# Top-k attention into an exact-GELU MLP: v's loads divided over the DMA queue, and three products of the last rows moved inside their slots

## The chip, the cores and the metric

The kernel runs on one core of a Trainium2 chip. The metric is the device time of one execution in microseconds (us). Five engines work side by side, each on its own list of instructions in order: TensorE (PE in the profile, with weight loads as PEld), VectorE (DVE), ScalarE (ACT), GpSimd (POOL) and SyncE (SP), which in this kernel issues nearly all DMAs. Waits between engines are semaphores. The time before is the median of three runs, 1484.7 us (1484.23 to 1486.39).

## The reference

```python
# q, k, v: (8, 8, 576, 64) float32;  w_in: (512, 2048);  w_out: (2048, 512)
scores = (q @ k.transpose(0, 1, 3, 2)) / np.sqrt(64)
kth = np.partition(scores, -32, axis=-1)[..., -32:-31]
scores = np.where(scores >= kth, scores, -1e9)
attn = np.exp(scores - scores.max(-1, keepdims=True))
attn = attn / (attn.sum(-1, keepdims=True) + 1e-9)
x = (attn @ v).transpose(0, 2, 1, 3).reshape(4608, 512)
h = x @ w_in
out = (0.5 * h * (1.0 + erf(h / np.sqrt(2.0)))) @ w_out
```

Each row of 576 scores keeps its 32 largest, the softmax runs over these, the result is multiplied with v, and the 4608 rows of all heads go through an MLP with exact GELU. All of it is float32.

## The kernel before

**Items and slots.** The heads of a batch are taken in four pairs. The 576 query rows of a pair are cut into four blocks of 128 rows (t = 0 to 3, "main") and 64 rows left over. The left-over rows of two pairs make one item together (t = 4, "last rows"). So a batch has 16 main items and 2 items of last rows, and the kernel has 144 items. In an even batch the last rows stand at the end, in an odd batch at the beginning, so four items of last rows follow one another: 16, 17, 18, 19, then 52 to 55, 88 to 91 and 124 to 127. The list `starts` holds the first item of each batch (54, 90 and 126 among them).

The main loop is software-pipelined over slots n = 0, 1, 2, ... . Slot n computes the scores of item n + 2 or n + 3 (`scores`, TensorE, copied out by ScalarE), finds the 32nd largest of item n (`top_k`, VectorE: MAX8 and MATCH_REPLACE8), masks and exponentiates item n - 1 (`softmax`, ScalarE, with its select at line 532 and its exponential at line 544), normalises item n - 1 (`normalise`, GpSimd, line 567), turns P of item n - 2 so that keys stand on partitions, multiplies P with v for an item some slots back (`attend`), and runs pieces of the MLP (`mlp`) in between.

**Two ways to turn P.** Most odd items are turned by TensorE (`transposes`, tiles tp and tp_t, copied to tile pt by ScalarE). From item 27 on, the last rows and most even items are `squared`: VectorE turns 32 x 32 squares in place (`square_p`, line 591), four DMAs write the item to a DRAM tile turned (`write_p`, line 601), and four DMAs read it back into pt (`read_p`, line 611). All of them are issued by SyncE in the order of the program. Tile pt has one buffer and holds two items side by side, the even one in the first half of its columns. A read for an even item therefore needs the products of the two items before it done. `delayed(i)` is true for squared last rows: items 52 to 55, 88 to 91 and 124 to 127.

**The products.** `attend(i)` multiplies pt with v. For main rows (line 727) one product covers two items, 256 columns. For last rows (line 738) it covers one item: two pairs of heads, 40 matmuls of 64 columns. The four products of a group of last rows are called first to fourth here (items 52, 53, 54, 55 in the first group). The result stands in a PSUM bank o and is copied to xT by ScalarE (lines 732 and 748). In this part of the kernel o, t_ps, tp_t and seven take turns in one single bank (tag "z"), so each waits until ScalarE has emptied the one before. Before the change the third and fourth product share one bank o and are copied to xT together.

Where the products stand before the change: the first at the beginning of slot 56 (n - 4 = 52), the second in slot 57 behind `softmax`, the third and fourth one after the other in slot 59, behind three pieces of the MLP. Slot 60 has the product of items 56 and 57.

**v.** Four buffers raw_v hold the v of four pairs; v0 to v3 stand for them here. The first product uses v0 and v1 for the last time in an even batch, the second v2 and v3; the third and fourth use what is loaded into these buffers for the next batch. One pair's `load("v", ...)` is four DMAs (lines 134 and 138). `issue` holds them back: in a slot with `held` set they go out at `flush()`, behind `write_p`.

**The MLP.** `l1_piece` (line 790) multiplies xT with w_in into h_ps; `gelus` applies GELU on ScalarE (line 806), with a table load because softmax's exponential needs another table; `sums` makes sums of GELU's output on GpSimd (lines 827 to 830). The second product of the MLP is done in seven products per pair of units: `seven_piece` (line 944, tile seven) and six in `trio_piece` (line 946, tiles y_ps). A "piece" is one entry of the list that `mlp` works through in order.

The slot's order around the change, shortened:

```python
mid = [i for i in (n - 5, n - 4) if delayed(i) and n % 2 and (i % 2 or i in starts)]
if not mid:
    read_p(n - 3)
...
if delayed(n - 4) and n % 2 == 0 and n - 4 not in starts:
    product = attend(n - 4)
...
if few[0]:
    softmax(n - 1, 0)
    if len(mid) == 1:
        mids()          # slot 57: second product, then read_p(54)
    if n % 2:
        mlp(ODD)        # ODD = 2 pieces
    if len(mid) == 2:
        mlp(1)
        mids()          # slot 59: third and fourth product, then read_p(56)
```

Of the kernel before, what the change touches and what calls it, by code (L numbers as in the profile page):

```python
# [14 lines left out]
def kernel(  # L15
# [19 lines left out]
    nc = tc.nc  # L35
# [5 lines left out]
    B, H, S, D = q.shape  # L41
# [4 lines left out]
    NP = H // 2  # L46
    NM = S // P
    SM = NM * P
    TL = S - SM
# [44 lines left out]
            return raws[n][pair % 2 if pair < SQUARES else 0]  # L94
        return raws[n][pair % len(raws[n])]

    held, late_issues = [False], []

    def issue(f):

        if held[0]:
            late_issues.append(f)
        else:
            f()
# [146 lines left out]
    items, starts = [], []  # L251
# [22 lines left out]
    def bank(name):  # L274

        tag = "z" if few[0] else ("z", "y0", "y1", "y2")[turn[0] % 4]
        turn[0] += 1
        return ps.tile([P, 512], f32, tag=tag, bufs=1, name=name)
# [298 lines left out]
    def delayed(i):  # L577

        return squared(i) and items[i][1] == NM
# [111 lines left out]
    def copy_x():  # L691
        while copies:
            copies.pop()()
# [2 lines left out]

    copies = []

    shared = []

    def column(tok):

        at = tok % RING
# [2 lines left out]
    def attend(i):  # L706

        if i < 0 or i >= N:
            return False
        pair, t = items[i]  # L710
        b, at = divmod(pair, NP)
        if t < NM and t % 2 == 0:
            return False
        pt = pt_now[0]
        both = delayed(i) and i - 1 in starts
        o = shared.pop() if both else bank("o")
        off = 2 * TL if both else 0
        n, row = (2 * P, (t - 1) * P) if t < NM else (TL, SM)
        tok = place_of(b, row)
        gap = RING if t == NM else COLS if tok % RING >= COLS else RING - COLS  # L720
        assert read[0] >= tok - gap + n
        c = slice(column(tok), column(tok) + n)
        if t < NM:
            vt = raw_of("v", pair)
            for j in range(NJ):
                for e in range(2):
                    nc.tensor.matmul(  # L727
                        o[e * D : (e + 1) * D, 0:n], lhsT=vt[:, j, e, :],
                        rhs=pt[:, e * NJ + j if j < NM else NM, :],
                        start=(j == 0), stop=(j == NJ - 1),  # L730
                    )
            copies.append(lambda: nc.scalar.copy(out=xT[:, at, c], in_=o[:, 0:n]))
        else:
            for r in range(2):
                vt = raw_of("v", pair + r)
                for j in range(NJ):
                    for e in range(2):
                        nc.tensor.matmul(
                            o[e * D : (e + 1) * D, off + r * TL : off + (r + 1) * TL],
                            lhsT=vt[:, j, e, :],  # L740
                            rhs=pt[:, e * NJ + j if j < NM else NM, i % 2 * P :][:, half(r, e)],
                            start=(j == 0), stop=(j == NJ - 1),
                        )
            if delayed(i) and i in starts:
                shared.append(o)
            else:
                first = 0 if both else at
                copies.append(lambda: nc.scalar.copy(
                    out=xT[:, first : at + 2, c],
                    in_=o[:, 0 : off + 2 * TL].rearrange("p (r n) -> p r n", n=TL),  # L750
                ))

        if t == (NM if b % 2 == 0 else NM - 1):
            for r in range(2 if t == NM else 1):
                issue(lambda r=r: load("v", pair + r + NP))
        if at == (NP - 1 if t < NM else NP - 2):
            assert n_tok[0] == tok
            n_tok[0] = tok + n
        return True
# [414 lines left out]
    for n in range(ahead):  # L1174

        held[0] = n < N and squared(n - 2)
        mid = [i for i in (n - 5, n - 4) if delayed(i) and n % 2 and (i % 2 or i in starts)]
        if not mid:
            read_p(n - 3)

        def mids():
            for i in mid:
                attend(i)
            copy_x()
            read_p(n - 3)
        left[0] = room_in(n)
        few[0] = n > START + 2
        eager[0] = n > N
        left[0] += closes(n - 3) - closes(n - 2)
        if not waits(unit_in(n)):  # L1190
            weights_add(unit_in(n))
        if n > 0:
            larger(n + 1)
        for piece in squares_in.pop(n, []):
            piece()
        if n == 1:

            for e in range(2):
                select(0, e)
            for e in range(2):  # L1200
                softmax(0, e)
        two = few[0] and n % 2 == 0 and n + 3 < N and items[n + 3][1] < NM
        scores(n + 2, two)
        if two:
            scores(n + 3)
        if delayed(n - 4) and n % 2 == 0 and n - 4 not in starts:
            product = attend(n - 4)
        else:
            product = not delayed(n - 3) and attend(n - 3)
        late = n > START  # L1210
        if n != 1 and n < START:

            for e in range(2):
                select(n - 1, e)
            softmax(n - 1, 0)
        copy_x()
        if n == START:

            for e in range(2):
                select(n - 1, e)  # L1220
            softmax(n - 1, 0)
        if waits(unit_in(n)):
            weights_size(unit_in(n))
            weights_add(unit_in(n))
        mlp(1)
        if closes(n - 3):
            ready[0] = n_tok[0]
        if few[0] and n % 2:
            run_gelus()
        tr = transposes(n - 2)  # L1230
        if product and n > START and done[0] < len(pieces) and pieces[done[0]][0] > ready[0]:

            for piece in tr[:1]:
                piece(n + 2 if few[0] else None)
            tr, ready[0] = tr[1:], n_tok[0]
        if not few[0] and n > START:
            softmax(n - 1, 0)
        mlp(1)
        if n != 1 and not late:
            softmax(n - 1, 1)  # L1240
        if few[0]:
            softmax(n - 1, 0)
            if len(mid) == 1:
                mids()
            if n % 2:
                mlp(ODD)
            if len(mid) == 2:
                mlp(1)
                mids()
        mlp(1)  # L1250
        prep = prep_in.pop(n, [])
        if n == 0:
            weights_size(unit_in(1))
            keep_busy(14, ident)
        if n == START + 1:

            for piece in prep:
                piece(None)
            prep = []
        if len(prep) > 1 and len(tr) == 3:  # L1260
            tr, prep = tr[:1] + prep[:1] + tr[1:], prep[1:]
        now = tr[:-1]
        if few[0]:
            now, tr, prep = tr + prep[:1], [], prep[1:]
        for x, piece in enumerate(now):
            piece(n + 2 if few[0] else None)
            ready[0] = n_tok[0]
            if few[0] and x == 2:
                break
            mlp(1)  # L1270
        ready[0] = n_tok[0]
        if late:
            softmax(n - 1, 1)
        if n > 0:
            smaller(n + 1)
        add_small(n - 1)
        for piece in tr[-1:] + prep:
            piece(None)
            mlp(1)
        if n < START:  # L1280

            keep_busy(4 if n == 0 else 8 if product else 14 if n < 5 else 18, ident)

        run_gelus()
        mlp(left[0])
        run_gelus()
        if n < N:
            top_k(n, lambda: inverse(n - 1), lambda: square_p(n - 2))
            write_p(n - 2)
            flush()  # L1290
            if n == 0:
                larger(1)
        else:
            inverse(n - 1)
        threshold(n)
        if n == 0:
            smaller(1)
        normalise(n - 1)
        sum_up(n + 2)
        if n in sums_in:  # L1300
            weight_sums(sums_in[n])
        run_small(6)

        if n > 0 and not waits(unit_in(n + 1)):
            weights_size(unit_in(n + 1))
        run_stores()
        if n == N:
            run_stores()
        for m in (n + 1, n + 2):

            if m > 2 and waits(unit_in(m)) == (m == n + 1):
                load_weights(m)
        if n < NP:
            load("v", n)
        if n == 5:
            nc.vector.memset(flat["k"][0][TL:, 0:TL], 0.0)
            load("q", SQUARES)
            load("k", SQUARES)
# [38 lines left out]
```

## Time and profile before

| | before |
|---|---|
| median of 3 runs | 1484.7 us (1484.23 to 1486.39) |
| the profiled execution: time, span | 1488.04 us, 1486.3 us |
| mean granted TensorE clock | 0.996 |
| busy share: PE, PEld, DVE, ACT, POOL | 98%, 77%, 88%, 73%, 77% |
| DMA writes of P (turned) / reads of P (pt), issues of 144 KB each | 240 / 240 |
| DMA loads of v, issues | 64 of 128 KB, 64 of 16 KB |

How to read the profile. A row of the timeline gives the start in us from the span's start, the length, the engine, the line of the kernel, the operation with its tiles (out<-in) and how many instructions are merged in it; brackets give the engine's idle time ahead of it and what ended that. SPq is SyncE's queue: its rows are the issues of DMAs, not the transfers. A row of the windows gives, for each stretch, its length, the busy time of each engine, the granted clock (1.00 is full speed) and the DMA engines' share. Buffer numbers are left out of tile names. A wait for several semaphores is put down to the one that came last.

### The profile page before, as it was taken

To read this page: it belongs to the slowest core of one execution; us is meant where nothing else is said; L and a number is where in the kernel's file an instruction comes from. 1 tells how busy PE (TensorE), PEld (TensorE's weight loads), DVE (VectorE), ACT (ScalarE), POOL (GpSimd) and SP (SyncE) were. 2 spreads that over 40 slices of the span, in tenths; PEclk is the share of its full clock that TensorE was granted. 3 is DMA by queue.
4 is the path that set the end of the run, shared out by engine and by line. 5 is a ranking of instruction groups with operands and counts; after the bars stand their busy time and mean duration, and the time that the engine had idled before them with its cause. 6 is when DMAs were issued, how large, how long until landed. Compare 5 with 4: busy or idle time off the path is not lost. (4 is left out here: it accounts for less than half of the span.)

```text
span 1486.3 us, 26513 instructions
## 1 busy us (share of the span) xinstructions
PE 1453.6 (98%) x8693; PEld 1137.4 (77%) x8693; DVE 1307.9 (88%) x3331; ACT 1081.5 (73%) x1899; POOL 1141.0 (77%) x1290
## 2 busy tenths in 40 slices
PE   8999999999999998999999999999999999899998
PEld 6776677887777776887777777787777777687787
DVE  7999899999999998899999999799999999898701
ACT  7999877877777775777777777677777777677620
POOL 6877567778888878777898978687788888877632
PEclk9999999999999999999999999999999999999999
DMA  7425210055434355245534337344443424623300
GB/s 195 144 86 131 76 47 1 23 100 100 88 82 86 62 108 128 59 95 112 104 79 85 72 67 155 67 94 96 97 101 74 88 63 93 130 60 73 66 15 15
DMA packets 544714, 127.05 MB, mean 85 GB/s; under 512 B 466464, under 2 KB 536128, under 8 KB 544576
## 3 DMA queue, kind: packets, MB, share of 16 engines
q1 hardware_dynamic: 543312, 124.93, 39.4%
q8 instruction: 69, 1.13, 0.3%
q14 instruction: 69, 0.57, 0.1%
q10 hardware_dynamic: 1200, 0.39, 0.1%
q0 software_dynamic: 64, 0.03, 0.0%
HBM read 80.47 MB, written 44.83 MB: 84 GB/s over the span
## 5 line engine op out<-in xcount | busy, mean ns | idle before, releaser
L790 PE MATMUL h_ps<-xT,w_in_sb 128*128 128x256 f32 (+1 forms) x2560 | 533.9, 361 | 0.0
L790 PEld LDWEIGHTS h_ps<-xT,w_in_sb 128*128 128x128 f32 x2560 | 438.5, 191 | 73.4 <-issue 25.5
L498 DVE MAX8 top<-lists 128x8 f32<-128x576 f32 (+1 forms) x792 | 475.8, 640 | 0.0
L501 DVE MATCH_REPLACE8 lists<-top,lists 128x288 f32<-128x288 f32 (+1 forms) x528 | 307.8, 589 | 0.0
L567 POOL TENSOR_TENSOR s<-s,stat 128x1152 f32<-128x1152 f32 x135 | 285.9, 2117 | 0.3 <-DVE stat L519 0.3
L532 ACT ACTIVATE s<-s,stat 128x576 f32<-128x576 f32 x288 | 224.9, 790 | 19.3 <-POOL stat L512 19.2
L544 ACT ACTIVATE s<-s,stat 128x576 f32<-128x576 f32 x288 | 225.0, 785 | 11.6 <-POOL lists L462 0.7
L525 POOL TENSOR_SCALAR stat<-stat 128x2 f32<-128x2 f32 x144 | 31.4, 218 | 218.7 <-ACT s L544 204.6
L470 POOL TENSOR_TENSOR lists<-lists 128x576 int32<-128x576 int32 x132 | 186.2, 1411 | 4.0
L462 POOL TENSOR_TENSOR lists<-s 128x576 int32<-128x576 int32 x133 | 187.6, 1411 | 0.0
L727 PE MATMUL o<-pt,raw_v 128*64 128x256 f32 x1280 | 154.0, 386 | 6.2 <-DMA pt<-turned 4.4
L727 PEld LDWEIGHTS o<-pt,raw_v 128*64 128x64 f32 x1280 | 87.6, 137 | 91.1 <-issue 44.1
L806 ACT ACTIVATE g<-h_ps 128x512 f32<-128x512 f32 x144 | 78.2, 595 | 108.7 <-PE h_ps L790 108.5
L946 PE MATMUL y_ps<-w_out_sb,sum 128*128 128x256 f32 x472 | 141.1, 381 | 0.0
L410 ACT ACTIVATE s<-s_ps 128x1024 f32<-128x1024 f32 x127 | 125.3, 1032 | 8.8 <-PE s_ps L402 8.2
L402 PE MATMUL s_ps<-kt,qm 64*128 64x512 f32 x512 | 129.4, 618 | 0.8 <-ACT s L408 0.8
L672 ACT COPY pt<-tp 128x1024 f32<-128x1024 f32 x73 | 74.3, 1018 | 57.5 <-PE tp L657 57.4
L501 DVE MATCH_REPLACE8 lists<-first,lists 128x288 f32<-128x288 f32 x264 | 114.3, 439 | 0.0
L946 PE MATMUL y_ps<-w_out_sb,g 128*128 128x256 f32 x480 | 113.7, 380 | 0.0
L519 DVE RECIPROCAL stat<-stat 128x2 f32<-128x2 f32 x144 | 22.9, 159 | 102.6 <-POOL stat L525 101.8
L498 DVE MAX8 first<-lists 128x8 f32<-128x288 f32 x268 | 106.6, 436 | 0.0
L437 DVE TENSOR_TENSOR lists<-s 128x576 f32<-128x576 f32 x133 | 101.0, 760 | 0.0
(162 smaller groups left out, 2489.0 us busy)
## 6 DMA issues: line engine op xcount, KB each, us to landing
turned<-s SPq DMA_DIRECT2D x240, 144.0 KB, 3.6
pt<-turned SPq DMA_DIRECT2D x240, 144.0 KB, 3.2
raw_v<-in_v_dram SPq DMA_DIRECT2D x64, 128.0 KB, 2.6
raw_q<-in_q_dram SPq DMA_DIRECT2D x112, 72.0 KB, 2.4
raw_k<-in_k_dram SPq DMA_DIRECT2D x112, 72.0 KB, 2.4
out_dram<-y SPq DMA_DIRECT2D x30, 256.0 KB, 2.1
w_out_sb<-in_moe_w_in_dram SPq DMA_DIRECT2D x14, 511.8 KB, 4.8
w_out_sb<-in_moe_w_out_dram SPq DMA_DIRECT2D x10, 511.8 KB, 4.1
```

Source lines behind the costliest of these rows:

```text
L402: nc.tensor.matmul(s_ps[:, e], lhsT=q_t[rows, :], rhs=kt[rows, main_keys(pair)], start=True, stop=True)
L410: nc.scalar.activation(spread(s, S + TL, SM), s_ps, func=AF.Copy, scale=scale)
L462: nc.gpsimd.tensor_tensor(t[:, :, 1].bitcast(i32), a.bitcast(i32), b.bitcast(i32), op=ALU.add)
L470: nc.gpsimd.tensor_tensor(into_of(i)[:, :, 1].bitcast(i32), both, top, op=ALU.subtract)
L498: nc.vector.max(x[:, e], src[:, e])
L501: nc.vector.match_replace(dst[:, e], x[:, e], src[:, e], LOWEST)
L532: nc.scalar.activation(s, s, func=AF.Prelu, bias=st["neg"][:, e : e + 1], scale=1.0, alpha=STEEP)
L544: nc.scalar.activation(s, s, func=AF.Exp, bias=st["bias"][:, e : e + 1], scale=1.0, accum_out=st["den"][:, e : e + 1],)
L567: nc.gpsimd.tensor_tensor(s, s, wide, op=ALU.mult)
L727: nc.tensor.matmul(o[e * D : (e + 1) * D, 0:n], lhsT=vt[:, j, e, :], rhs=pt[:, e * NJ + j if j < NM else NM, :], start=(j == 0), stop=(j = ...
L790: nc.tensor.matmul(h_tile(u)[:, i, :], lhsT=w_in_sb[:, ko, f * P : (f + 1) * P], rhs=xT[:, ko, c0 : c0 + n], start=(ko == 0), stop=(ko == ...
L946: nc.tensor.matmul(acc[names][:, k], lhsT=lhsT, rhs=rhs, start=(j == 0 and k == 0), stop=(j == FT // 2 - 1 and k == 1),)
```

## The change

In the slots of last rows (56, 57 and 59, and their like in the other two groups):

- v0's loads, and v2's, go out right behind the product that used the buffer last (`soon`, `issue_soon`), and not behind the write of P at the slot's end. v1's and v3's stay there. In slot 56 the read of P of item 53 now stands behind the first product and v0's loads; in slot 57 v2's loads stand behind the read of item 54.
- The second product (slot 57) stands behind two more pieces of the MLP (`mlp(ODD)`).
- The third product (slot 59) stands at the slot's beginning, in front of the last four h matmuls of its unit and of seven. The fourth stands behind two pieces, where three were.
- The third and fourth product no longer share a bank; each is copied to xT by itself.

On SyncE's queue the order per group was: write 53, read 53, write 54, v0, v1, read 54, write 55, v2, v3, stores, read 55, write 56, read 56. It is now: write 53, v0, read 53, write 54, v1, read 54, v2, write 55, v3, stores, read 55, write 56, read 56. TensorE runs the same matmuls; ScalarE has one copy more per group.

```diff
-    held, late_issues = [False], []
+    held, late_issues, soon = [False], [], []
+
+    def issue_soon():
+        while soon:
+            soon.pop()()
...
-        both = delayed(i) and i - 1 in starts
-        o = shared.pop() if both else bank("o")
-        off = 2 * TL if both else 0
+        o = bank("o")
...
-            if delayed(i) and i in starts:
-                shared.append(o)
-            else:
-                first = 0 if both else at
-                copies.append(lambda: nc.scalar.copy(
-                    out=xT[:, first : at + 2, c],
-                    in_=o[:, 0 : off + 2 * TL].rearrange("p (r n) -> p r n", n=TL),
-                ))
+            copies.append(lambda: nc.scalar.copy(
+                out=xT[:, at : at + 2, c],
+                in_=o[:, 0 : 2 * TL].rearrange("p (r n) -> p r n", n=TL),
+            ))
...
             for r in range(2 if t == NM else 1):
-                issue(lambda r=r: load("v", pair + r + NP))
+                f = lambda r=r: load("v", pair + r + NP)
+                if r == 0 and delayed(i):
+                    soon.append(f)
+                else:
+                    issue(f)
...
-        if not mid:
+        even_last = delayed(n - 4) and n % 2 == 0 and n - 4 not in starts
+        if not mid and not even_last:
             read_p(n - 3)
 
         def mids():
-            for i in mid:
-                attend(i)
-            copy_x()
-            read_p(n - 3)
+            attend(mid.pop(0))
+            if not mid:
+                copy_x()
+                read_p(n - 3)
+                issue_soon()
...
-        if delayed(n - 4) and n % 2 == 0 and n - 4 not in starts:
+        if even_last:
             product = attend(n - 4)
+            issue_soon()
+            read_p(n - 3)
         else:
             product = not delayed(n - 3) and attend(n - 3)
+        if len(mid) == 2:
+            mids()
...
             softmax(n - 1, 0)
-            if len(mid) == 1:
-                mids()
             if n % 2:
                 mlp(ODD)
-            if len(mid) == 2:
-                mlp(1)
-                mids()
+                if mid:
+                    mids()
```

More of the change, by code (lines that the diff above doesn't have):

```diff
@@ L697 @@
     copies = []
-    shared = []
     def column(tok):
@@ L738, in attend @@
                         nc.tensor.matmul(
-                            o[e * D : (e + 1) * D, off + r * TL : off + (r + 1) * TL],
+                            o[e * D : (e + 1) * D, r * TL : (r + 1) * TL],
                             lhsT=vt[:, j, e, :],
```

## The prediction

> **What bounds the kernel now.** I read the page's first part, then stages by windows, then TensorE's timeline where it waits.
>
> ```profile
> PE 1453.6 (98%) x8693; PEld 1137.4 (77%) x8693; DVE 1307.9 (88%) x3331; ACT 1081.5 (73%) x1899; POOL 1141.0 (77%) x1290
> ```
>
> ```profile
> 600.00:890.00 290.00, 289.56 (x1648) 226.89 (x1647) 272.32 (x702) 217.25 (x385) 237.47 (x266) 1.00 0.43 84
> 589.00:595.60 6.60, 6.60 (x33) 4.80 (x34) 6.60 (x15) 1.91 (x4) 6.52 (x8) 0.74 0.36 56
> 932.00:942.10 10.10, 10.09 (x71) 7.72 (x71) 2.83 (x7) 3.44 (x8) 0.71 (x1) 0.69 0.40 88
> 1291.00:1296.00 5.00, 5.00 (x33) 3.96 (x34) 5.00 (x14) 1.96 (x5) 4.92 (x5) 1.00 0.01 3
> ```
>
> Columns: stretch, its length, busy time of PE, PEld, DVE, ACT and POOL, granted clock, DMA. Between two groups of last rows TensorE is busy 289.56 of 290.00 us: what it gains inside a group isn't given back behind it. In two of the three groups the clock falls (0.74, 0.69). The change touches slots 56, 57 and 59 and their like (items 52 to 55, 88 to 91, 124 to 127). TensorE in the first group:
>
> ```profile
> 544.91 1.39 PE L738 MATMUL o<-pt,raw_v 128*64 128x64 f32 x40
> 555.06 1.39 PE L738 MATMUL o<-pt,raw_v 128*64 128x64 f32 x40 [0.58 <-ACT y L962]
> 559.30 0.49 PE L367 MATMUL t_ps<-kt,qm 128*128 128x128 f32 x2
> 565.42 6.21 PE L790 MATMUL h_ps<-xT,w_in_sb 128*128 128x256 f32 x28
> 572.63 1.13 PE L944 MATMUL seven<-w_sum,g 128*128 128x256 f32 x4 [1.00 <-POOL g L829]
> 573.60 1.89 PE L946 MATMUL y_ps<-w_out_sb,g 128*128 128x256 f32 x8
> 575.32 0.59 PE L946 MATMUL y_ps<-w_sum,sum 128*128 128x256 f32 x2
> 578.90 1.39 PE L738 MATMUL o<-pt,raw_v 128*64 128x64 f32 x40 [1.24 <-DMA pt<-turned]
> 580.22 0.70 PE L946 MATMUL y_ps<-w_sum,sum 128*128 128x256 f32 x2
> 581.18 0.38 PE L367 MATMUL tp_t<-kt,qm 128*128 128x128 f32 x2
> 588.95 3.47 PE L727 MATMUL o<-pt,raw_v 128*64 128x256 f32 x20 [2.75 <-DMA pt<-turned]
> ```
>
> 544.91, 555.06 and 578.90 are the first, second and fourth product; the third stands just before the fourth. 588.95 is the product of items 56 and 57, the first after the group. Four waits: 0.58, 1.00, 1.24, 2.75. The other groups:
>
> ```profile
> 923.98 1.13 PE L944 MATMUL seven<-w_sum,g 128*128 128x256 f32 x4 [0.99 <-POOL g L829]
> 932.01 2.40 PE L738 MATMUL o<-pt,raw_v 128*64 128x64 f32 x40 [2.99 <-DMA pt<-turned]
> 942.16 2.38 PE L727 MATMUL o<-pt,raw_v 128*64 128x256 f32 x20
> 1275.53 1.13 PE L944 MATMUL seven<-w_sum,g 128*128 128x256 f32 x4 [0.99 <-POOL g L829]
> 1282.09 1.39 PE L738 MATMUL o<-pt,raw_v 128*64 128x64 f32 x40 [1.51 <-DMA pt<-turned]
> 1290.99 2.38 PE L727 MATMUL o<-pt,raw_v 128*64 128x256 f32 x20 [1.61 <-DMA pt<-turned]
> ```
>
> The waits for P sum to 1.24 + 2.75 + 2.99 + 1.51 + 1.61 = 10.10 us. Who makes P late is in the DMA queue's own timeline, first group:
>
> ```profile
> 541.61 3.70 SPq L601 DMA_DIRECT2D turned<-s  x4
> 547.94 2.54 SPq L611 DMA_DIRECT2D pt<-turned  x4
> 550.71 3.54 SPq L601 DMA_DIRECT2D turned<-s  x4
> 554.36 0.78 SPq L134 DMA_DIRECT2D raw_v<-in_v_dram  x1
> 560.55 2.78 SPq L611 DMA_DIRECT2D pt<-turned  x4
> 563.43 3.37 SPq L601 DMA_DIRECT2D turned<-s  x4
> 566.85 0.95 SPq L134 DMA_DIRECT2D raw_v<-in_v_dram  x1
> 572.50 1.00 SPq L861 DMA_DIRECT2D out_dram<-y  x2
> 573.56 2.59 SPq L611 DMA_DIRECT2D pt<-turned  x4
> 576.26 3.42 SPq L601 DMA_DIRECT2D turned<-s  x4
> 583.78 2.54 SPq L611 DMA_DIRECT2D pt<-turned  x4
> ```
>
> These are write 53, read 53, write 54, eight loads of v (v0, v1), read 54, write 55, eight loads (v2, v3), stores, read 55, write 56, read 56. From 550.71 to 576.26 the queue issues without a break, so issuing, not moving, makes read 55 late; eight loads cost 560.55 - 554.36 = 6.19 or 572.50 - 566.85 = 5.65, four about 2.9. Before read 53 it stands free from 545.31 to 547.94: read 53 waits for write 53 to land.
>
> **The change part by part.** In the changed program the order per group is: write 53, four loads (v0), read 53, write 54, four (v1), read 54, four (v2), write 55, four (v3), stores, read 55, write 56, read 56. As many issues as before; 24 of them, four loads in each of six places, stand earlier.
>
> *v0's loads* wait on the queue for the first half of the first product (544.91 + 0.66 = 545.6); read 53 and write 54 stand behind them. They fill 545.7 to about 548.6, mostly the free stretch, so read 53 starts 0.7 us later; write 54, which needs VectorE's square only, moves from 550.71 to about 551.4. v1's follow to 557.9. Read 54 needs write 54 landed (read 53 followed its write by 547.94 - 541.61 = 6.33: 557.7) and the second product done, since P's buffer is single (below: 557.5): it starts near 557.9, not 560.55. v2's loads come at 560.7, write 55 stays at about 563.6, v3's run from 567.0 to 569.8, and after 1.06 for the stores read 55 goes at 570.8 instead of 573.56. I take 2.8 us; nothing if landings set it instead, 3.5 if the free stretch covers all of v0's.
>
> *Second product behind two pieces.* It stops waiting 0.58 for the bank behind ScalarE's copy, and the eight y matmuls (575.32 - 573.60 = 1.72) go first: TensorE 554.48 + 1.72 = 556.2, done 557.5. But t_ps, two pieces later, needs the same bank, which ScalarE frees in this row:
>
> ```profile
> 559.00 0.24 ACT L748 COPY xT<-o 128x128 f32<-128x128 f32 x1
> 569.83 1.28 ACT L806 ACT_TABLE_LOAD   x1
> 571.66 1.08 ACT L806 ACTIVATE g<-h_ps 128x512 f32<-128x512 f32 x2 [0.55 <-PE h_ps L790]
> 573.80 0.37 ACT L965 COPY p<-seven 128x256 f32<-128x256 f32 x1 [1.05 <-PE seven L944]
> 578.46 0.78 ACT L544 ACTIVATE s<-s,stat 128x576 f32<-128x576 f32 x1
> ```
>
> That copy stands behind an exponential that TensorE doesn't set. So t_ps stays at 559.30 and the 0.58 turns up there: I take 0 (bounds 0 and 0.58 per group).
>
> *Third product at its slot's beginning.* It needs read 54, landed some 7 us earlier. Its 1.32 us (580.22 - 578.90) go in front of the last four h matmuls: 24/28 of 6.21 ends at 570.74, the product at 572.06, h at 572.95. seven could not start before 572.6 (it waits for GpSimd's sums), and now starts at 572.95: 1.32 done for 0.32, a gain of 1.00 (bounds 0.7 and 1.0). Its price is on ScalarE: a copy of 0.24, which waits for the product, with table load, Gelu and the copy of seven queued behind it: 572.3, 573.6, 574.7, 575.1. The fourth product, which now takes a bank of its own, needs that last copy; TensorE is there at 572.95 + 2.69 (572.63 to 575.32) = 575.6. Hidden by 0.5; beyond that it would cost one for one. The extra copy itself (two of 0.24 for one of 0.37) is covered by ScalarE's idle time.
>
> *Fourth product behind two pieces.* Between the first issue of its read and its start lay 578.90 - 573.56 = 5.34 us in the first group; the others are bounded by these rows:
>
> ```profile
> 924.89 2.83 SPq L611 DMA_DIRECT2D pt<-turned  x4
> 1275.97 3.41 SPq L611 DMA_DIRECT2D pt<-turned  x4
> ```
>
> that is 7.12 and 6.12. So it starts at 570.8 + 5.34 to 7.12 = 576.1 to 577.9, ends 577.4 to 579.2, and one pair of y matmuls (580.22 to 581.18: 0.96) leads to tp_t at 578.4 to 580.2. tp_t needs the bank again, and the fourth product's copy stands behind the exponential of 578.46: 579.24 + 0.25, so 579.5 at the earliest. I take 579.6: a new wait of 0.6 or so on ScalarE, beside some 1.1 left of the one for P. tp_t stood at 581.18, but one pair that preceded it now follows: net 0.6. From tp_t until TensorE was ready for the next product it was 588.95 - 2.75 - 581.18 = 5.02, now 5.98: ready at 585.6.
>
> *Read 56.* Write 56 follows read 55 by 2.70 (573.56 to 576.26): 573.5. Read 56 followed it by 7.52, another read its write by 6.33: 579.8 to 581.0. From there to the product 588.95 - 583.78 = 5.17: 585.0 to 586.2. I take 585.8 for both conditions: 588.95 - 585.8 = 3.15 us.
>
> *The clock.* After waits of 2.75 and 2.99 the clock was halved for part of the next stretch; after 1.51 and 1.61 it wasn't. The stretches 589.00:595.60 and 1291.00:1296.00 above hold the same 33 instructions: 6.60 at 0.74 against 5.00 at 1.00, 1.60 us. From the fourth product to readiness for the next: 942.16 - 932.01 = 10.15 against 1290.99 - 1.61 - 1282.09 = 7.29: 2.86. The waits left are about 1.1, 0.6 and 0.2, each shorter than 1.61, so I take both back (bounds: nothing, and 4.46).
>
> [...]
>
> Sum. First group 3.15 + 1.60 = 4.8. Second, shifted by 923.98 - 572.63 = 351.35: the next product at 937.15 instead of 942.16, 5.0, the clock in it. Third, shifted by 702.90: 1288.7 instead of 1290.99, 2.3. Together 12.1 us. The profiled execution took 1488.04 (span 1486.3 and 1.7 around it), 3.3 above the median of 1484.7; the gain is the same for both: **1484.7 - 12.1 = 1472.6**. The most that could go is 10.10 + 2.98 (seven) + 1.74 (0.58 thrice) + 4.46 = 19.3: 1465.4.
>
> **The rivals.** (1) *The clock still halves*: the remaining waits lie within some 4 us, and if their sum counts, 4.5 stay, and the third group may add 1.6: 1477.1 to 1478.7. For it: two groups halve now; against: the third, with waits of 0.99, 1.51 and 1.61, doesn't. (2) *The reads don't come earlier*, because landings, not issuing, set the queue: write 55 can't leave earlier than VectorE and v2's loads allow, and read 55 needs it landed. Then only the third product's 1.0 per group is gained: 1481.7. For it: read 56 followed its write by 7.52; against: 10 us without a break up to read 55. (3) *Slower*: loads that wait for TensorE stand at the head of the one queue. Place: v0's loads before read 53. The second product starts at 556.2, so read 53 must go by 551.0 (landing 5.17) or 549.1 (7.12); it is planned at 548.6. Beyond that point every microsecond delays the second product, with it read 54, write 55 and all that follows. At twice the issue time (5.8 for four) read 53 goes at 551.5, the second product waits up to 2.4, the queue's 2.8 are gone, and three groups lose 3 x (2.4 - 1.0) = 4.2: 1488.9. Against it: no four loads in these rows took over 3.1.
>
> **How the numbers follow.** Forecast 0.60 (1468 to 1476, from the bounds of its terms), rival 1 0.17, rival 2 0.11, rival 3 0.12. The range runs from 1467.5, near all that the waits hold, to 1481.5, with rival 1 in it and rival 2 at its edge. 0.2% is 3 us, about what a measurement of this kernel can tell from no change. Faster by more: forecast, rival 1 and a little of rival 2, 0.79; within: the rest of rival 2, 0.10; slower 0.11.
>
> **What would show it.** Right: read 55 about 3 us sooner after write 53; no wait at seven; none of 2.7 for P at the product after a group; new waits on ScalarE's xT copy at t_ps (0.5) and tp_t (about 0.6); clock 1.00 behind all groups; 290 us between groups unchanged. Wrong: the fourth product or the next still waits over 2 us for P, the second product waits for P, or the fourth waits for the copy of seven.

## The result, and the profile after

Five runs of the changed kernel: median 1478.31 us (1477.45 to 1479.42). The kernel before, five runs of the same comparison: 1485.9. The ratio is 0.9953, with a 95% interval of 0.9938 to 0.9967, so the change gains 7.6 us. Forecast were 1472.6 us and a gain of 12.1, with a range from 1467.5 to 1481.5. The profiled execution of the changed kernel took 1479.29 us (span 1477.5), 8.75 less than that of before.

TensorE's timeline in the first group of the changed kernel (start, length, engine, line, operation, tiles, count; in brackets the idle time ahead and what ended it):

```profile
544.77 1.39 PE L738 MATMUL o<-pt,raw_v 128*64 128x64 f32 x40
556.00 1.39 PE L738 MATMUL o<-pt,raw_v 128*64 128x64 f32 x40
559.19 0.49 PE L371 MATMUL t_ps<-kt,qm 128*128 128x128 f32 x2 [0.74 <-ACT xT L744]
...
570.58 1.39 PE L738 MATMUL o<-pt,raw_v 128*64 128x64 f32 x40
572.86 1.03 PE L944 MATMUL seven<-w_sum,g 128*128 128x256 f32 x4
576.82 1.39 PE L738 MATMUL o<-pt,raw_v 128*64 128x64 f32 x40 [1.21 <-DMA pt<-turned]
579.41 0.49 PE L371 MATMUL tp_t<-kt,qm 128*128 128x128 f32 x2
...
587.31 1.05 PE L727 MATMUL o<-pt,raw_v 128*64 128x256 f32 x7 [1.91 <-DMA pt<-turned]
...
592.31 0.39 PE L371 MATMUL t_ps<-kt,qm 128*128 128x128 f32 x2
```

The second product (556.00) no longer waits, and t_ps waits for ScalarE's copy instead; the third product stands at 570.58, and seven behind it doesn't wait. All of that is as forecast. The product after the group starts at 587.31, where 588.95 stood before and 585.8 was forecast. First, fourth and next product of the other two groups, after; then the first products of the same groups, before:

```profile
893.04 1.39 PE L738 MATMUL o<-pt,raw_v 128*64 128x64 f32 x40
...
926.13 1.39 PE L738 MATMUL o<-pt,raw_v 128*64 128x64 f32 x40 [2.25 <-DMA pt<-turned]
934.81 2.38 PE L727 MATMUL o<-pt,raw_v 128*64 128x256 f32 x20 [0.52 <-DMA pt<-turned]
1240.46 1.39 PE L738 MATMUL o<-pt,raw_v 128*64 128x64 f32 x40
...
1273.51 2.12 PE L738 MATMUL o<-pt,raw_v 128*64 128x64 f32 x40 [2.20 <-DMA pt<-turned]
1283.18 2.38 PE L727 MATMUL o<-pt,raw_v 128*64 128x256 f32 x20
```

```profile
896.27 1.39 PE L738 MATMUL o<-pt,raw_v 128*64 128x64 f32 x40
1247.83 1.39 PE L738 MATMUL o<-pt,raw_v 128*64 128x64 f32 x40
```

A group's gain is read from its first product to the product after it, so that what earlier groups gained doesn't count twice: 44.04 to 42.54, 45.89 to 41.77, 43.16 to 42.72. That is 1.50, 4.12 and 0.44. In the first group 1.6 comes on top behind that product, since the clock no longer halves there (from 587.31 to the next t_ps at 592.31 it takes 5.00 us at a clock of 1.00; the same stretch before the change, 588.95 to 595.60, took 6.65 at a clock of 0.74). Together 7.7 of the two executions' 8.8. The last 1.0 comes behind the third group and is spread: from the product after that group to the end of the span it is 195.3 us before and 194.3 after, and between 194.3 and 195.6 in the profiled executions of all kernels here, without following the change. In the third group the fourth product took 2.12 us instead of 1.39. The windows of the changed kernel (length, busy time of PE, PEld, DVE, ACT, POOL, granted clock, DMA) show the clock there, and between the groups:

```profile
600.00:888.00 288.00, 287.54 (x1639) 225.16 (x1637) 270.26 (x697) 215.67 (x382) 235.70 (x265) 1.00 0.43 85
926.10:930.00 3.90, 3.87 (x55) 3.58 (x56) 3.90 (x12) 2.17 (x6) 3.35 (x3) 1.00 0.68 107
1273.50:1277.40 3.90, 3.89 (x45) 3.48 (x46) 3.90 (x12) 1.66 (x4) 3.36 (x3) 0.56 0.66 103
```

Between groups TensorE is as full as before. SyncE's queue in the first group, after, from write 54 on:

```profile
551.09 3.33 SPq L605 DMA_DIRECT2D turned<-s  x4
554.52 0.93 SPq L138 DMA_DIRECT2D raw_v<-in_v_dram  x1
555.55 0.78 SPq L142 DMA_DIRECT2D raw_v<-in_v_dram  x1
556.39 0.58 SPq L138 DMA_DIRECT2D raw_v<-in_v_dram  x1
557.08 0.52 SPq L142 DMA_DIRECT2D raw_v<-in_v_dram  x1
558.10 3.15 SPq L615 DMA_DIRECT2D pt<-turned  x4
561.30 0.60 SPq L138 DMA_DIRECT2D raw_v<-in_v_dram  x1
561.95 0.52 SPq L142 DMA_DIRECT2D raw_v<-in_v_dram  x1
...
563.76 3.27 SPq L605 DMA_DIRECT2D turned<-s  x4
...
571.48 2.60 SPq L615 DMA_DIRECT2D pt<-turned  x4
574.19 3.39 SPq L605 DMA_DIRECT2D turned<-s  x4
581.88 2.54 SPq L615 DMA_DIRECT2D pt<-turned  x4
```

These are write 54, v1's loads, read 54, the first two of v2's, write 55, read 55, write 56 and read 56. Against the first product of each group, with the other groups read from the same view and the forecast's times taken from 544.91:

| us behind the first product | before, group 1 | forecast | after, groups 1, 2, 3 |
|---|---|---|---|
| read 53 | 3.03 | 3.7 | 3.64, 3.50, 3.32 |
| write 54 | 5.80 | 6.5 | 6.32, 6.18, 6.01 |
| read 54 | 15.64 | 13.0 | 13.33, 13.99, 14.09 |
| write 55 | 18.52 | 18.7 | 18.99, 19.07, 19.16 |
| read 55 | 28.65 | 25.9 | 26.71, 27.07, 27.68 |
| read 56 | 38.87 | 34.9 to 36.1 | 37.11, 36.57, 36.70 |
| product after the group | 44.04 | 40.9 | 42.54, 41.77, 42.72 |

Up to write 54 the queue runs as forecast or a little ahead of it. Read 54 is 0.3 to 1.1 us late, of which 0.3 to 0.5 is left at write 55; from write 55 to read 55 another 0.5 to 1.3 is lost. Read 55 comes 1.94, 1.55 and 0.46 us earlier than in the same group of before (28.65, 28.62 and 28.14), where 2.8 were forecast.

### The profile page after: what moved, and what is told of

It is laid out like the page before. It is cut to its first block, busy times and chain, and to the rows that moved or that the text cites. A ratio compares the mean times of both kernels' runs of the same rounds, so it can differ in the third digit from the quotient of the medians.

```text
span 1477.5 us, 26521 instructions
## 1 busy us (share of the span) xinstructions
PE 1449.7 (98%) x8693; PEld 1134.6 (77%) x8693; DVE 1307.8 (89%) x3331; ACT 1082.8 (73%) x1902; POOL 1142.0 (77%) x1290
```

## The experiments

A DMA lands when its data has arrived; its landing is the time from its issue to that. Theory T: the order of issues on SyncE's one queue sets when P comes, P sets when the product after the group starts, and the moves of the three products are worth nothing. Rival M: the moves are worth about 1.0 us per group by themselves. The times stand against the kernel before on the same chip (1487.38, 1487.51 and 1487.41 us in the three series). The first series has the loads early without moves, the moves alone, ScalarE's queue and the stores; the third has all of v early and v3 behind read 55; the second has the rest.

| run | median, us | ratio to before (95%) | read 55, us behind the first product, groups 1, 2, 3 |
|---|---|---|---|
| the changed kernel again | 1479.09 | 0.9946 (0.9932 to 0.9960) | 26.74, 26.96, 27.40 |
| loads early, no moves | 1478.53 | 0.9946 (0.9930 to 0.9961) | 26.37, 25.92, 26.60 |
| moves alone | 1489.28 | 1.0011 (1.0001 to 1.0020) | 28.65, 29.51, 29.32 |
| only v0 early | 1480.67 | 0.9954 (0.9940 to 0.9968) | 26.86, 26.64, 27.72 |
| only v2 early | 1487.28 | 1.0002 (0.9993 to 1.0010) | 29.43, 28.91, 28.90 |
| all of v early | 1491.46 | 1.0031 (1.0019 to 1.0043) | 30.24, 31.12, 29.26 |
| v1, v3 on ScalarE's queue | 1498.03 | 1.0064 (1.0049 to 1.0078) | 30.81, 30.97, 33.77 |
| stores behind write 58 | 1476.08 | 0.9919 (0.9906 to 0.9932) | 25.43, 26.26, 25.66 |
| the same, no moves | 1476.03 | 0.9926 (0.9910 to 0.9941) | 25.78, 25.82, 25.54 |
| stores as there, v3 behind read 55 | 1476.51 | 0.9927 (0.9915 to 0.9940) | 23.14, 23.57, 23.17 |

The edits below are against the changed kernel.

**Loads early, no moves.** The bank shared by the third and fourth product is back as well, and `mids` does all products of `mid` at once (not shown).

```diff
-        if len(mid) == 2:
-            mids()
...
             softmax(n - 1, 0)
+            if len(mid) == 1:
+                mids()
             if n % 2:
                 mlp(ODD)
-                if mid:
-                    mids()
+            if len(mid) == 2:
+                mlp(1)
+                mids()
```

> Only v0's and v2's loads go out early; the three products stand where they stood before the change, and the third and fourth share a bank again. Theory T (the time is set by the order of issues on SyncE's queue, read 55 -> write 56 -> read 56, and the product after the group follows read 56 by some 5.3 us): the queue has the same order as in the changed kernel, so read 55 and read 56 come as early, the product after the first group starts at 587 to 588 us as in the changed kernel (587.31), and nearly the whole gain of 7.6 us remains: 1477.5 to 1480 where the kernel before takes 1485.9. seven keeps its 1.0 us wait, but TensorE would have waited for P anyway. Rival M (the moves are worth about 1.0 us per group by themselves, the third product in the wait of seven): the gain is about 3 us smaller than the change's, 1481 to 1482, and the product after the first group starts near 588.3.

The ratio is that of the changed kernel, 0.9946. TensorE's timeline, third and fourth product (one row of 80 matmuls) and the one after the group:

```profile
576.08 2.55 PE L742 MATMUL o<-pt,raw_v 128*64 128x64 f32 x80
...
586.99 2.38 PE L731 MATMUL o<-pt,raw_v 128*64 128x256 f32 x20 [2.43 <-DMA pt<-turned]
```

The fourth product no longer waits for P, because it stands later; the wait is whole at the next product, and that starts 42.28 us behind the first product against 42.54. seven's 1.0 and the bank's 0.58 are back and cost nothing that shows: the product after the group starts 42.28, 41.41 and 41.85 behind the first, against 42.54, 41.77 and 42.72 in the changed kernel. Rival M doesn't fit these rows. The intervals of the two ratios alone would leave room for some 3 us (an estimate from their widths); the next run settles it.

**Moves alone.** All loads go out behind the write of P, as before the change.

```diff
-                if r == 0 and delayed(i):
-                    soon.append(f)
-                else:
-                    issue(f)
+                issue(f)
...
-        if not mid and not even_last:
+        if not mid:
             read_p(n - 3)
...
-            issue_soon()
-            read_p(n - 3)
```

> Only the three products are moved; all of v's loads go out behind the write of P as before the change. Theory T: read 55 goes out when it did before (28.1 to 28.7 us behind the first product), so P of item 55 comes as late, and what the third product gains at seven is waited for by the fourth (over 2 us for P instead of 1.2 to 3.0); the product after the group starts within 0.5 us of where it stood before (588.95 in the first group). Time 1484.5 to 1487, no gain beyond 1 us. Rival M: 1.0 us per group is gained all the same, 1482 to 1483, and the product after the first group starts near 587.9.

No gain, as theory T had it, and a small loss, which neither expected. The fourth products of the second and third groups:

```profile
931.20 2.40 PE L738 MATMUL o<-pt,raw_v 128*64 128x64 f32 x40 [4.45 <-DMA pt<-turned]
...
1282.46 2.40 PE L738 MATMUL o<-pt,raw_v 128*64 128x64 f32 x40 [4.24 <-DMA pt<-turned]
```

What the third product gains ahead of seven is waited for here, in one piece. In all three groups the product behind the wait takes 2.40 us at a granted clock of 0.50 (windows of 4.68 to 4.80 us from its start), where it takes 1.39 at 1.00; before the change it took 1.39 in the first and third. The third group shows the price: its product after the group starts 45.70 us behind the first, where 43.16 stood before.

**Stores moved.** The two stores between v3's loads and read 55 go out behind write 58.

```diff
-        run_stores()
+        if not (delayed(n - 4) and n % 2 or delayed(n - 5) and n % 2 == 0 and n - 4 in starts):
+            run_stores()
```

> The changed kernel with the two stores of the output, which stand between v3's loads and read 55 on SyncE's queue, moved behind write 58 (three times in the run). Theory T: read 55, write 56 and read 56 go out 0.7 to 1.7 us earlier (the stores' issue time, 1.06 in the first group, 1.74 in the third); the wait of the fourth product for P (1.21, 2.25 and 2.20 us) shrinks by that, the third group's halved clock goes, and the time falls by 1.5 to 4 us, to 1474.5 to 1477. Rival L (landings, not issues, set the end: read 56 followed write 56 by up to 7.69 us): read 55 goes out earlier, but read 56 does not, and the time stays at 1478 within 1 us.

**The same without the moves of the products.**

> v0's and v2's loads early and the stores behind write 58, as in the run with the stores moved, but the three products where they stood before the change (third and fourth together behind three pieces, in one shared bank). Theory T: read 55 and read 56 go out as early as with the stores moved (570.13 and 580.39 in its first group), so the product after the group starts within 0.5 us of its 585.66, and the time is its 1476.1 within 1.5 us: the moves are worth nothing with P early either. Rival M: with P early the third product's 1.0 us at seven counts at last, and this kernel, without the moves, is 2 to 3 us slower than with them: 1478 to 1479.

Both medians are 3 us below the changed kernel's 1479.09. Of the kernel with the moves no run (1474.96 to 1476.71) is as slow as the fastest of the changed kernel (1477.45); of the six without them two are (1477.93 and 1479.80). The two are equal within their spread, though their intervals would leave room for some 4 us (an estimate from their widths). The first group of the one with the moves, SyncE's queue:

```profile
570.13 2.64 SPq L615 DMA_DIRECT2D pt<-turned  x4
```

and TensorE:

```profile
575.61 1.39 PE L738 MATMUL o<-pt,raw_v 128*64 128x64 f32 x40
579.32 0.49 PE L371 MATMUL tp_t<-kt,qm 128*128 128x128 f32 x2 [1.27 <-ACT xT L744]
...
585.66 2.38 PE L727 MATMUL o<-pt,raw_v 128*64 128x256 f32 x20 [0.35 <-DMA pt<-turned]
```

Read 55 is 1.3 us earlier than in the changed kernel's first group, the fourth product's wait for P is gone there, and the product after the group stands 40.96 us behind the first, at the forecast's 40.9. The time gained at the fourth product turns up as a wait of 1.27 at tp_t, behind the copy that stands behind the exponential. In the other two groups the fourth product still waits, 1.91 and 1.34 us, and tp_t doesn't. Without the moves the product after the group starts 40.04, 41.14 and 41.23 behind the first product (40.96, 41.51 and 41.01 with them): by these rows the moves gain nothing even where P comes earlier.

**Only v0's loads early.**

```diff
-                if r == 0 and delayed(i):
+                if r == 0 and delayed(i) and i % 2 == 0:
```

> The changed kernel, but only v0's loads go out early; v2's stand behind write 55 again, with v3's. Theory T (write 55 cannot go before VectorE's square, near 563.3, whatever stands ahead of it): SyncE's queue stands idle between read 54 and write 55, the eight loads and the stores stand behind write 55 as before the change, and read 55 goes out where it did before (28.1 to 28.7 us behind the first product, not 26.7 to 27.7): the gain is gone, and the time is that of the moves alone, 1487 to 1490. Rival H (each of the two early groups of loads is worth half): 1482 to 1484.

This refutes a part of theory T, and rival H too: v0's loads alone give nearly the whole gain, at 1480.67 us against 1479.09. SyncE's queue:

```profile
557.54 3.35 SPq L615 DMA_DIRECT2D pt<-turned  x4
560.99 3.69 SPq L605 DMA_DIRECT2D turned<-s  x4
...
571.45 2.60 SPq L615 DMA_DIRECT2D pt<-turned  x4
```

and VectorE's square of item 55, which write 55 needs:

```profile
559.39 1.36 DVE L595 STREAM_TRANSPOSE s<-s 128x1152 f32<-128x1152 f32 x1
```

The square is done at 560.75, so write 55 follows read 54 at once, 16.40 us behind the first product and not 19.0. In the changed kernel it is v2's loads that hold it back, not VectorE. From read 54 to read 55 the queue issues the same things nearly without a break in either order, in 13.1 to 14.2 us here and 13.1 to 13.6 in the changed kernel. So v2's loads gain nothing that shows by standing ahead of write 55; what gains is that v0's fill the stretch ahead of read 53.

**Only v2's loads early.**

```diff
-                if r == 0 and delayed(i):
+                if r == 0 and delayed(i) and i % 2:
```

> The changed kernel, but only v2's loads go out early; v0's stand behind write 54 again, with v1's. Theory T: eight loads behind write 54 keep read 54 at about 560.5, v2's four follow, so write 55 goes out at about 566 and not 563.4, and read 55 where it did before the change: no gain from the loads, 1487 to 1490 as with the moves alone. Rival H (each half is worth half): 1482 to 1484.

As expected: read 54 goes at 561.15 in the first group, write 55 is pushed to 566.51, read 55 is no earlier than before, and the time is that of before.

Theory T2, from here: the stretch ahead of read 53 holds four loads; what counts is when read 54 goes and how much is issued between it and read 55.

**All of v's loads early.** v0 and v1 behind the first product, v2 and v3 behind the second.

```diff
-        soon.pop()()
+        soon.pop(0)()
...
-                if r == 0 and delayed(i):
+                if delayed(i):
```

> All of v's loads early: v0 and v1 right behind the first product, v2 and v3 right behind the second; the order is write 53, v0, v1, read 53, write 54, read 54, v2, v3, write 55, stores, read 55. Theory T2 (the free stretch ahead of read 53 holds four loads and no more; what counts is when read 54 goes and how many issues stand between it and read 55): read 53 goes at 6.3 to 6.5 us behind the first product's start (3.3 to 3.7 in the changed kernel), the second product waits 0.3 to 1 us for P, read 54 follows at 15.4 to 16.5 (13.3 to 14.1), write 55 at 24 to 25 and, with nothing to fill its landing, read 55 at 30.5 to 31.5 (26.7 to 27.7). The fourth product then waits 5 us or more for P and the clock halves: slower than before the change, 1490 to 1496. Rival E (the earlier the loads the better): 1475 to 1478.

Slower than before, as T2 had it. SyncE's queue and the fourth product of the first group:

```profile
550.24 2.58 SPq L615 DMA_DIRECT2D pt<-turned  x4
552.93 3.44 SPq L605 DMA_DIRECT2D turned<-s  x4
560.68 2.53 SPq L615 DMA_DIRECT2D pt<-turned  x4
...
568.10 3.70 SPq L605 DMA_DIRECT2D turned<-s  x4
```

```profile
580.35 2.12 PE L738 MATMUL o<-pt,raw_v 128*64 128x64 f32 x40 [4.91 <-DMA pt<-turned]
```

Between write 54's end (556.37) and read 54 the queue now stands free for 4.3 us, since nothing is left to issue while write 54 lands. All eight loads of v2 and v3 stand between read 54 and write 55, so the landing of write 55 has only the stores to fill it, and the queue stands free again, for 1.5 to 2.2 us ahead of read 55. The second product, expected to wait 0.3 to 1 us, starts 11.24 to 11.36 us behind the first, against 11.23 without a wait.

**v3's loads behind read 55**, with the stores moved and v2's loads back behind write 55.

```diff
-                if r == 0 and delayed(i):
+                if r == 1 and delayed(i) and i % 2:
+                    after_read.append(f)
+                elif r == 0 and delayed(i) and i % 2 == 0:
                     soon.append(f)
...
             read_p(n - 3)
+            while after_read and n % 2 == 0:
+                after_read.pop(0)()
```

> The changed kernel with the stores behind write 58, and two more moves: v2's loads back behind write 55, v3's behind read 55. Only v0's stay early. Theory T2: write 55 goes at 16.4 us behind the first product, as in the run with v0's loads alone early, read 55 at about 23 (25.4 to 26.3 with the stores moved), so the fourth product no longer waits for P; but write 56 stands at 28.5 where it was at 28.2 to 29.3, so the product after the group, which waits for read 56, comes no earlier: 1476 within 1 us of the run with the stores moved. Rival F (the fourth product's wait for P, 1.9 and 1.3 us in two groups, is on the path): 1473 to 1474.

Read 55 comes 2.3 to 2.7 us earlier than with the stores alone moved, and the fourth product waits for P in no group. The time is the same, as T2 had it:

```profile
575.45 1.39 PE L738 MATMUL o<-pt,raw_v 128*64 128x64 f32 x40
579.31 0.49 PE L371 MATMUL tp_t<-kt,qm 128*128 128x128 f32 x2 [1.42 <-ACT xT L744]
...
585.31 2.38 PE L727 MATMUL o<-pt,raw_v 128*64 128x256 f32 x20
```

tp_t stands where it stood (579.31 against 579.32): its bank comes free behind the fourth product's copy, which follows the exponential. tp_t waits 1.42 us for the copy in all three groups. The product after the group waits 0, 0.86 and 0.22 us for P of item 56. By these waits the copy and read 56 are the limits now, within a microsecond of one another, and taking away a third that lies ahead of both gained nothing; no run takes one of these two away.

**v1's and v3's loads on ScalarE's queue.**

```diff
-                    issue(f)
+                    issue((lambda r=r: load("v", pair + r + NP, nc.scalar)) if delayed(i) else f)
```

> The changed kernel with v1's and v3's loads (eight issues per group) on ScalarE's DMA queue, in place of SyncE's. Theory T: SyncE's queue is freed of 5.8 us of issues per group, read 55 goes out up to 4 us earlier, until write 55's landing sets it; the waits for P at the fourth product (1.21, 2.25, 2.20) and at the product after the group (1.91, 0.52, none) go, 1472 to 1475. Counter-mechanism: an issue on ScalarE's instruction list takes ScalarE's time; where eight issues cost it 4 to 6 us per group between softmax and the copies xT<-o, t_ps and the copies queue behind them, and the time rises above the changed kernel's, to 1480 or more.

Slower than the kernel before by 0.64%, and not mainly by the mechanism expected: of that the first group shows 1.32 us, for which ScalarE stands idle behind v1's issues, ahead of its table load at 552.14. Both queues in the first group:

```profile
552.19 0.51 SPq L142 DMA_DIRECT2D raw_v<-in_v_dram  x1
552.80 2.57 SPq L615 DMA_DIRECT2D pt<-turned  x4
```

```profile
549.96 0.38 ACTq L138 DMA_DIRECT2D raw_v<-in_v_dram  x1
```

```profile
SPq L142 <- DMA raw_v<-in_v_dram: 4.8, 1, 4.8
```

The last row is from the waits of SyncE's queue between 540 and 556 us: the fourth load of v0 waits 4.8 us for another load of v. v1's four loads go out on ScalarE from 549.96 on. Its first should land near 552.3, an estimate from the 2.3 us (median) in which such loads landed there, and v0's fourth goes out on SyncE at 552.19; v0's third, issued at 546.78 and with 3.1 us to landing by the same view, should have landed near 549.9. By these times it is v1's first load that SyncE's queue waits for. Why a load on one queue should hold up another queue isn't shown. With v0's fourth load read 53 is held up; the load is late in all three groups (it goes 7.64, 7.64 and 8.41 us behind the first product, and 2.96, 2.83 and 2.60 in the changed kernel). Read 53 goes at 8.25 instead of 3.64, the second product waits 2.42 us for P, and the fourth 3.90 to 4.21; it then takes 2.26 to 2.40 us where it takes 1.39 at a clock of 1.00, and in the first group the clock is 0.68 from 580.70 to 586.00. The time is 1498.03 us against 1487.38.

## Why the prediction came out as it did

*The total*: the time lies in the stated range, but in part by chance. It is outside the 1468 to 1476 of the forecast's own terms and in the 1477.1 to 1478.7 of the first rival, whose mechanism is at most a small part of what happened: the clock came back in the two groups where it had fallen (1.00, where 0.74 and 0.69 stood), and halved newly in the third group of one of two profiled executions. That 7.6 us is also the sum without the clock's 4.5 is chance in the same way. What is missing is the queue's, as the next paragraphs show.

*What bounds the groups*: right. The product after the group follows P, P follows the queue, and moving the loads alone gives the whole gain.

*Read 55 earlier by 2.8 us*: the direction right, the size wrong. This is the term that is mis-sized: 1.94, 1.55 and 0.46 us. Two of its parts were too short. Read 54 was put some 6.5 us behind write 54 (551.4 to 557.9); it took 7.01, 7.81 and 8.08, with v1's loads in between. From write 55 to read 55 the forecast had 7.2 us; it took 7.72, 8.00 and 8.52, since v3's loads, right behind a write, took 3.2 and not 2.8 in the first group, and the stores between 1.0 and 1.7 (three groups). The 3.2 could have been read before the change: the four loads right behind write 55 took it there too (566.85 to 570.02), so the forecast's "no four loads in these rows took over 3.1" is a little low.

*v2's loads*: the forecast has write 55 "at about 563.6", and there it is. That v2's loads standing ahead of it are themselves the reason, and gain nothing, wasn't seen; it costs the sum nothing, since the queue is busy either way.

*Second product*: right. The 0.58 went to t_ps as 0.74, and the gain is nothing.

*Third product*: right that seven's 1.00 goes, in all three groups, and right that it isn't in the sum. Rival 2, though, priced it at 1.0 per group if P comes no earlier. The moves alone show that price to be wrong: they lose 1.9 us (1489.28 against 1487.38, the ratio's interval just above 1), for what is gained is waited for at the fourth product in one piece, and the clock falls to 0.50 in three groups.

*Fourth product and tp_t*: the wait of "some 1.1 left" for P was 1.21, 2.25 and 2.20. The wait of tp_t on ScalarE's copy wasn't there, since the product came too late for it; with the stores moved it appears in the first group, at 1.27.

*Read 56*: write 56 to read 56 took 7.69, 6.07 and 6.31, where the forecast had 6.33 to 7.52: one a little above, two a little below. It took 5.43 and 5.20 from there to the product in the first two groups. The forecast's 40.9 us to the product after the group was missed by 1.65, 0.89 and 1.85, together 4.4, which is what the profiled executions' 7.7 lacks of the 12.1. In the changed kernel's second profiled execution it was missed by 1.4, 1.4 and 0.7, so up to 1.2 us of a group's figure is spread.

*The clock*: right in the first two groups. In the third group of the profiled execution it halves newly (0.50 from 1274.0 to 1277.2), which the first rival had put at 1.6 for "the third group may add"; from the fourth product to tp_t that group takes 3.86 us against 2.28 in the second. Part of it would have been waited for P anyway. In the second profiled execution of the same kernel the fourth product of that group waits 1.97 us and takes 1.39, at a clock of 1.00, so the halving there isn't fixed to the kernel.

*The slower rival*: its condition didn't arise in the changed kernel, where read 53 goes at 548.41. Its mechanism shows on ScalarE's queue: there read 53 goes at 552.80, past both of its limits (549.1 and 551.0), and the second product waits 2.42 us, where it had up to 2.4. It isn't the only way to be slower. With eight loads ahead of read 53 this read goes at 550.24, between the limits, and the second product is held up by 0.13 us at most; the kernel is slower all the same, because the landing of write 54 then passes with nothing to issue.

## What to carry to other kernels

In the changed kernel and in that with only v0's loads early SyncE's queue issued nearly without a break from read 54 to read 55 (13.1 to 14.2 us), and the order of what stood between the two changed nothing that could be measured (v2's loads ahead of write 55 or behind it: 1479.09 and 1480.67 us). The gains came from moving issues out of the busy stretch, into one where the queue waits for something to land (v0's loads, a ratio of 0.9954 alone) or behind the last read that matters (the stores, 1476.08 against 1479.09). Fill each landing with issues that nobody waits for, one landing's worth each: four loads ahead of read 53 gained, eight lost (1.0031). The moves alone put TensorE's work ahead into its waits while P came no earlier: the waits merged into one of 3.25 to 4.45 us at the fourth product, the clock behind it was 0.50, and the time rose from 1487.38 to 1489.28 us. Even with P earlier the moves showed no gain here (1476.08 with them, 1476.03 without).

## What the runs showed of the hardware that was not expected

- In the first group of the changed kernel issues took longer right behind a write of P (issues of 144 KB): v1's first two loads took 0.93 and 0.78 us behind write 54 and the next two 0.58 and 0.52; the first two of v2's, behind a read, took 0.60 and 0.52.
- With v1's and v3's loads on ScalarE's queue, SyncE's queue waited 4.8 us for a load of v, by the times above one that ScalarE had issued.
- No single length of TensorE's wait divides the waits with a lower clock behind them from those without in these runs. In the changed kernel a wait of 2.20 us was followed by a clock of 0.56, and one of 2.25 by 1.00 (windows above). With only v2's loads early, the third group's fourth product waited 3.69 us, and the windows of that kernel show the wait and then full clock:

```profile
1277.40:1281.10 3.70, 0.03 (x1) 0.01 (x1) 3.70 (x14) 2.92 (x4) 3.70 (x4) 1.00 0.93 202
1281.10:1289.00 7.90, 7.88 (x75) 6.07 (x75) 4.47 (x10) 3.84 (x8) 2.48 (x5) 1.00 0.56 121
```

By these rows the length of the wait alone doesn't decide; what does isn't shown.
